# An attention kernel whose K transposes get their lead in units 19 to 22 instead of 10 to 16, with a shorter warm-up

## The chip, the cores and the metric

One NeuronCore of one Trainium2 chip. The metric is the device time of one execution in microseconds (us). Every run also lists the span of the core, which is some 1.8 us shorter, and the mean granted clock of TensorE (PE), the share of full speed that it was given. "VectorE" is DVE in the profile, "ScalarE" ACT, "GpSimd" POOL.

## The reference, cut to what matters

```python
B, Sq, D = 8, 112, 640
H, Sk, Dh = 32, 512, 192                 # all bfloat16
q = (x @ wq).reshape(B, Sq, H, Dh).transpose(0, 2, 1, 3)
p = softmax(einsum("bhqd,bhkd->bhqk", q, k_cache) * Dh ** -0.5)
o = einsum("bhqk,bhkd->bhqd", p, v_cache)
return o.transpose(0, 2, 1, 3).reshape(B, Sq, H * Dh) @ wo
```

K and V are 50 MB each and are read once; the whole program reads 117.5 MB.

## The kernel before

It works in 64 units: 8 groups of 4 heads, times 8 batches. A unit is a score block S (96 matmuls), the transposes T of the output of the unit two before, and PV of the unit before. In two slots per unit, (i, 0) ahead of PV and (i, 1) behind it, stands dense work: Q projections of the next group, or output projections O. `halves` cuts one in two: over both slots of a unit, or over slot 1 and slot 0 of the next unit. VectorE transposes K, four quarters per unit, and adds the O results up. GpSimd copies V and reorders the Q weights. In the code below cuts are marked `# ...`; conditions for the first and last units are left out as well.

```python
    WARM, WN, BRIDGE, RAW = 7, 100, 4, 4
    # ... slots of group 0, and of the last group:
            put(6, 0, ("O", 0, 2))
            put(7, 1, ("O", 0, 3))
    # ...
            halves(i0 + 1, 0, ("O", g - 1, 5))
            put(i0 + 2, 0, ("O", g - 1, 6), FRONT)
            put(i0 + 3, 0, ("O", g - 1, 6), BACK)
    # ... how many quarters are transposed by the end of unit i: the lead is the min(5, ...)
        want = min(4 * (i + 2) + min(5, 1 + max(0, i - 8) // 2), 4 * NU)
    # ... VectorE, unit i
                for it in kts[:2]:
                    do_KT(*it)             # waits for all of K of its unit at its first quarter
                do_OEs(i, 0)               # adds of the O that ended in slot (i, 0)
                for it in kts[2:3]:
                    do_KT(*it)
                do_NM(i - 1)               # normalization
                do_OEs(i, 1)
                for it in kts[3:]:
                    do_KT(*it)
    # ... PE, first half of a projection: its two PSUM banks must have been read out
                        if q == 0:
                            bank_free(pe, pair, h)
                    if c == 0:             # first Q projection of a group: all its weights reordered
                        W(pe, gW, DC * g)
    # ... GpSimd: when the weights of group g >= 2 are reordered; then middle(u + NM) copies V
                    at.setdefault(8 * (g - 1) - 5 + dc if g >= 2 else -1, []).append((g, dc))
    # ... PE, before everything: a warm-up, and a bridge over a wait for ScalarE
            for j in range(WARM + 1):
                (held if j else pe.matmul)(ps[:, 7, 0:4 * WN], wt[:], warm, True, True)
            # ...
            for j in range(BRIDGE):
                (held if j else pe.matmul)(ps[:, 7, 0:128], wt[:], wt[:], True, True)
```

Of the kernel before, what the change touches and what calls it, by code (L numbers as in the profile page):

```python
# [666 lines left out]
def build_main(nc, x, k_cache, v_cache, wq, wo, out, flag, regs, hints):  # L667
# [4 lines left out]
    NU = NG * B  # L672
# [11 lines left out]
    RW = DH + 2  # L684
    FULL, FRONT, BACK = range(3)
    FILL = {}
    WARM, WN, BRIDGE, RAW = 7, 100, 4, 4
    HINT_AT = {"act": 55, "dve": 54, "pool": 40, "sp": 56}
    NM = 2
    KP = [4] * NU  # L690
# [63 lines left out]

    kt_ahead, done = [], 4
    for i in range(NU + 2):
        want = min(4 * (i + 2) + min(5, 1 + max(0, i - 8) // 2), 4 * NU)
        kt_ahead.append((done, want))
        done = max(done, want)

# [566 lines left out]
def bass_standalone__mha_block_cached__near_ridge_kernel(  # L1327
    nc: bass.Bass,
    x: bass.AP,
    k_cache: bass.AP,  # L1330
    v_cache: bass.AP,
    wq: bass.AP,
    wo: bass.AP,
    out: bass.AP,
):
    with nc.sbuf_tensor("flag", [1, 1], I32) as flag:
        regs, hints = {e: nc.alloc_register(e, "raised") for e in mybir.ALL_ENGINES}, {}
        build_main(nc, x, k_cache, v_cache, wq, wo, out, flag, regs, hints)
        for e, loc in hints.items():
            nc.engines[e].br_eq(regs[e], 0, on_true="main_end", on_false="main_again").branch_hint(loc)  # L1340
        with nc.body("main_again"):
            nc.all_engine_barrier()
            build_mha_kernel(nc, x, k_cache, v_cache, wq, wo, out)
            nc.br("main_end")
        nc.switch_bb("main_end")
    return nc
# [28 lines left out]
```

## Time and profile before

| | |
|---|---|
| time before, three runs known at the prediction | 393.70, 394.04, 394.27 us |
| span of the profiled execution | 392.8 us |
| granted clock | 1.00 |
| DMA share of most slices | 0.9 or more until 370 us |

The windows view gives the engines' busy time in stretches: start and end, length, then PE, weight loads (PEld), VectorE, ScalarE and GpSimd, each with its count of instructions in brackets, then the granted clock, the DMA share and GB/s. Besides the start and the end, these are the stretches of the kernel before in which PE is clearly not full.

```profile
50.00:60.00 10.00, 8.74 (x255) 6.54 (x246) 8.54 (x16) 5.97 (x13) 4.95 (x10) 1.00 0.97 322
100.00:110.00 10.00, 9.43 (x234) 5.58 (x217) 8.26 (x18) 4.70 (x11) 4.19 (x10) 1.00 1.03 358
360.00:370.00 10.00, 9.05 (x253) 6.23 (x241) 9.16 (x18) 6.25 (x14) 4.43 (x9) 1.00 0.98 341
```

What to see: PE is full nearly everywhere, and the change aims at the middle row, whose 9.43 hides one hole of 0.9 us.

### The profile page before, as it was taken

The numbers are of one execution on the slowest core, as the hardware profiler recorded it, in microseconds if no ns is written. First come the engines' busy times: TensorE is split into PE (matmuls) and PEld (weight loads), VectorE is DVE, ScalarE is ACT, GpSimd is POOL, SyncE is SP. The second block draws the span as 40 slices with busy tenths as digits, with TensorE's granted clock in tenths as the row PEclk, the third lists the DMA queues.
The fourth block names the chain that finished last, engine by engine and source line by source line (L and its number), as shares of the span: only waits on it lengthen the run. The fifth ranks groups of instructions, "written<-read, shape, count | busy, mean of one in ns | idle before, by whom it ended". The sixth has DMA issues, their size and how long they took to land.

```text
span 392.8 us, 19830 instructions
## 1 busy us (share of the span) xinstructions
PE 386.1 (98%) x8836; PEld 243.8 (62%) x8286; DVE 284.1 (72%) x506; ACT 250.5 (64%) x550; POOL 152.7 (39%) x352
## 2 busy tenths in 40 slices
PE   8999989999999999999999999999999999999997
PEld 4556666666566666666666656656666666666664
DVE  1666688688797777776787776876678676789835
ACT  3767755766556765666845666566774766666662
POOL 5442544335343354234342255233454233233331
PEclk9999999999999999999999999999999999999999
DMA  8999999999999999999998999989998889989812
GB/s 259 379 369 362 350 318 349 334 324 300 356 356 305 326 304 341 370 293 319 352 331 287 281 327 330 343 266 312 311 336 291 252 270 301 349 259 321 276 38 70
DMA packets 88584, 120.00 MB, mean 305 GB/s; under 512 B 9776, under 2 KB 88496, under 8 KB 88496
## 3 DMA queue, kind: packets, MB, share of 16 engines
q1 hardware_dynamic: 88496, 118.72, 90.8%
q8 instruction: 68, 1.11, 1.2%
q14 instruction: 20, 0.16, 0.1%
HBM read 117.54 MB, written 1.15 MB: 302 GB/s over the span
## 4 chain that ended last, share of the span: by engine, by line
PE 90%; DMA 5%; DVE 2%; issue 1%; ACT 0%; SPq 0%; DVEq 0%
PE ps L933 20%; PE ps L972 20%; PE ps L858 20%; PE ps L954 20%; PE ps L983 6%; DMA kr<-in_k_cache_dram 5%; PE ps L892 2%; DVE kt L1111 2%; DMA xs<-in_x_dram 1%; PE ps L877 1%; PE ps L854 1%; DVE acc L1131 0%; PE ps L897 0%; DVE acc L1134 0%; SPq L1314 0%
## 5 line engine op out<-in xcount | busy, mean ns | idle before, releaser
L1111 DVE STREAM_TRANSPOSE kt<-kr 128x384 int32<-128x384 int32 x256 | 196.2, 870 | 13.2 <-DMA kr<-in_k_cache_dram 13.1
L1052 ACT ACTIVATE pT<-ps 128x448 bf16<-128x448 f32 x256 | 130.8, 561 | 83.8 <-PE ps L954 83.8
L954 PEld LDWEIGHTS ps<-qT,kt 32*128 32x128 bf16 x6144 | 77.2, 93 | 31.3 <-issue 21.8
L933 PE MATMUL ps<-wos,oT 128*128 128x320 bf16 (+2 forms) x342 | 93.2, 299 | 0.5 <-DVE acc L1134 0.5
L972 PE MATMUL ps<-vm,pT 128*128 128x193 bf16 x768 | 91.5, 247 | 1.0 <-ACT oT L1069 0.8
L858 PE MATMUL ps<-wos,oT 128*128 128x320 bf16 x330 | 91.2, 299 | 0.1
L954 PE MATMUL ps<-qT,kt 32*128 32x112 bf16 x6144 | 88.1, 208 | 1.4 <-issue 1.1
L1231 POOL TENSOR_SCALAR bad<-rinv 112x4 f32<-112x4 f32 x64 | 14.6, 228 | 188.8 <-DVE rinv L1117 188.8
L1214 POOL COPY vm<-vs 128x1152 int32<-128x1152 int32 x64 | 73.4, 1147 | 26.2 <-issue 18.0
L972 PEld LDWEIGHTS ps<-vm,pT 128*128 128x128 bf16 x768 | 67.9, 97 | 22.0 <-ACT oT L1069 11.6
L933 PE MATMUL ps<-xT,wqs 128*128 128x448 bf16 x210 | 74.0, 352 | 0.0
L858 PE MATMUL ps<-xT,wqs 128*128 128x448 bf16 x210 | 73.9, 352 | 0.0
L1059 ACT ACTIVATE os<-ps,rinv 112x192 bf16<-112x192 f32 x128 | 47.8, 435 | 29.7 <-DVE rinv L1117 29.7
L972 PE MATMUL ps<-vs,pT 128*128 128x193 bf16 x256 | 62.6, 245 | 0.0
L933 PEld LDWEIGHTS ps<-wos,oT 128*128 128x128 bf16 x342 | 33.2, 97 | 43.8 <-issue 36.1
L1036 ACT ACTIVATE qT<-ps 128x448 bf16<-128x448 f32 x96 | 47.8, 554 | 17.8 <-PE ps L933 13.1
L1134 DVE TENSOR_TENSOR acc<-ps,acc 128x320 f32<-128x320 f32 x84 | 37.3, 485 | 25.1 <-PE ps L933 25.1
L1069 ACT ACTIVATE oT<-ps 128x672 bf16<-128x672 bf16 x64 | 46.4, 726 | 2.1 <-PE ps L983 2.1
L1117 DVE RECIPROCAL rinv<-ps 112x4 f32<-112x4 f32 x64 | 11.1, 173 | 47.5 <-PE ps L972 47.4
L933 PEld LDWEIGHTS ps<-xT,wqs 128*128 128x128 bf16 x210 | 20.4, 97 | 34.0 <-issue 29.1
L1120 DVE TENSOR_TENSOR os<-ps,rinv 112x384 bf16<-112x384 f32 x64 | 35.7, 558 | 7.4 <-DVE rinv L1117 0.5
L1207 POOL COPY wqs<-wqr 128x384 bf16<-128x384 bf16 x70 | 33.2, 506 | 5.0 <-DMA wqr<-in_wq_dram 5.0
(44 smaller groups left out, 155.7 us busy)
## 6 DMA issues: line engine op xcount, KB each, us to landing
kr<-in_k_cache_dram SPq DMA_DIRECT2D x256, 192.0 KB, 4.2
vs<-in_v_cache_dram SPq DMA_DIRECT2D x256, 192.0 KB, 4.0
wos<-in_wo_dram SPq DMA_DIRECT2D x48, 160.0 KB, 4.6
wqr<-in_wq_dram SPq DMA_DIRECT2D x35, 192.0 KB, 5.2
wqs<-in_wq_dram SPq DMA_DIRECT2D x5, 192.0 KB, 4.3
out_dram<-xs SPq DMA_DIRECT2D x6, 160.0 KB, 2.0
xs<-in_x_dram SPq DMA_DIRECT2D x2, 320.0 KB, 3.7
xs<-in_x_dram SPq DMA_DIRECT2D x1, 480.0 KB, 5.8
```

The lines of the kernel that those rows point to most:

```text
L858: return pe.add_instruction(mybir.InstMatmult(name=nc.get_next_instruction_name(), engine=mybir.EngineType.PE, ins=[pe.lower_ap_or_imm(rhs ...
L933: mm = (pe.matmul if h == hs[0] and f == 0 else held)(ps[:, bank_of(pair, h), cs], w, rhs[h][:, cs], q == 0, q == n - 1 and f == cuts - 1)
L954: mm = pe.matmul(ps[:, a, SQ * t:SQ * (t + 1)], kt[u % NT][p, t, c // 2, :, c % 2], qT[g % 2][p, c, SQ * b:SQ * (b + 1)], start=(c == 0), ...
L972: mm = pe.matmul(pv[:, k, e, 0:DH + 1], pT[u % 2][:, a, t, :], src[:, a, v0:v0 + DH + 1], start=(t == 0), stop=(t == 3), skip_group_check= ...
L1036: act.activation(qT[g % 2][:, c, HQ * h:HQ * (h + 1)], ps[:, bank_of_Q0(n) if g == 0 else 6 + h, 0:HQ], ACTF.Copy).then_inc(aQ, 1)
L1052: act.activation(pT[u % 2][:, a, :, 0:SQ], ps[:, a, 0:4 * SQ].rearrange("p (t q) -> p t q", t=4), ACTF.Exp, scale=scale).then_inc(aEX, 1)
L1059: ins = act.activation(os_[u % 2][:, DH * (2 + e):DH * (3 + e)], pv_of(u)[0:SQ, 1, e, 0:DH], ACTF.Copy, scale=rinv[:, u % 4, 2 + e:3 + e])
L1069: act.activation(oT[:, :, SQ * b:SQ * (b + 1)].rearrange("p (k c) q -> p k c q", k=2), src.rearrange("p k (c q) -> p k c q", c=3), ACTF.Co ...
L1111: dve.transpose(dst, src).then_inc(vKT, 1)
L1120: dve.tensor_tensor(os_[u % 2][:, 0:2 * DH].rearrange("p (e d) -> p e d", e=2), pv[0:SQ, 0, :, 0:DH], rinv[:, u % 4, 0:2][:, :, None].broa ...
L1134: ins = dve.tensor_tensor(ob[:, m, cs] if g == NG - 1 else acc[:, m, cs], src, acc[:, m, cs], op=ALU.add)
L1214: gp.tensor_copy(vm[u % NM][:].rearrange("p a (t w) -> p a t w", w=RW)[:, :, :, 0:DH].bitcast(I32), vs[u % NV][:, :, 32:32 + 3 * DH].rearr ...
```

## The change

The lead is how many quarters of K, beyond those of the next unit, VectorE has transposed. The intent is to raise it later, when K is well ahead, and to trim the warm-up.

```diff
-    WARM, WN, BRIDGE, RAW = 7, 100, 4, 4
+    WARM, WN, BRIDGE, RAW = 5, 128, 3, 4
...
-        want = min(4 * (i + 2) + min(5, 1 + max(0, i - 8) // 2), 4 * NU)
+        want = min(4 * (i + 2) + min(5, 1 + max(0, i - 18)), 4 * NU)
```

## The prediction

> **What bounds the kernel now.** I read the page first: its busy shares, its chain of work and its DMA rows.
>
> ```profile
> span 392.8 us, 19830 instructions
> ...
> PE 386.1 (98%) x8836; PEld 243.8 (62%) x8286; DVE 284.1 (72%) x506; ACT 250.5 (64%) x550; POOL 152.7 (39%) x352
> ...
> PE 90%; DMA 5%; DVE 2%; issue 1%; ACT 0%; SPq 0%; DVEq 0%
> ...
> L1111 DVE STREAM_TRANSPOSE kt<-kr 128x384 int32<-128x384 int32 x256 | 196.2, 870 | 13.2 <-DMA kr<-in_k_cache_dram 13.1
> ```
>
> TensorE (PE) has work for 386.1 of 392.8 us, at granted clock 1.0 throughout, and 90% of the chain is its matmuls. The matmuls are full: the timeline has the 320-column ones 0.135 us apart, which is 320 columns at 2.4 columns per ns. The change touches none of that work, so it can only win or lose in the small holes. The sum of the holes is an upper bound: 392.8 - 386.1 = 6.7 us, and most of that is start, end and fixed turns. The last row is what the change moves: 256 K transposes on VectorE (DVE), 4 per unit, about 0.77 us apart (4 take 3.0 us), with 13.1 us of DVE idling until K data lands.
>
> Next I took the windows view in 10 us stretches to find where PE is less than full: 8.48 in 0 to 10, 8.74 in 50 to 60, 9.43 in 100 to 110, 9.05 in 360 to 370, and 9.9 or more everywhere else. Then the timeline of each. The one in 100 to 110 lies in unit 15, where the old rule has just raised the lead to 4:
>
> ```profile
> 102.62 1.60 DVE L1111 STREAM_TRANSPOSE kt<-kr 128x384 int32<-128x384 int32 x2
> ...
> 105.13 1.57 DVE L1111 STREAM_TRANSPOSE kt<-kr 128x384 int32<-128x384 int32 x2 [0.91 <-DMA kr<-in_k_cache_dram]
> ...
> 106.34 0.24 PE L972 MATMUL ps<-vs,pT 128*128 128x193 bf16 x1
> 106.56 0.86 DVE L1134 TENSOR_TENSOR acc<-ps,acc 128x320 f32<-128x320 f32 x2
> ...
> 107.08 0.10 PEld L933 LDWEIGHTS ps<-wos,oT 128*128 128x128 bf16 x1 [0.72 <-DVE acc L1134]
> 107.08 0.31 PE L933 MATMUL ps<-wos,oT 128*128 128x320 bf16 x1 [0.49 <-DVE acc L1134]
> 107.35 0.83 DVE L1111 STREAM_TRANSPOSE kt<-kr 128x384 int32<-128x384 int32 x1
> 107.47 0.30 PE L858 MATMUL ps<-wos,oT 128*128 128x320 bf16 x1
> 107.61 0.30 PE L933 MATMUL ps<-wos,oT 128*128 128x320 bf16 x1
> ```
>
> Read it as a relay. DVE is free at about 104.2 but stands before two transposes of unit 17 whose K only lands at 105.1. Behind them in its order is the output add (L1134) that empties the two PSUM banks of one output projection; its input was ready at about 105.1, when PE finished that projection. The add therefore runs at 106.56 rather than 105.1, and PE, done with PV at 106.43, cannot begin the next projection, which uses the same banks. A lead meant to protect PE has made PE wait.
>
> [...] the ready add stood 1.4 us behind a transpose waiting for data. [...] That bears on three holes in the middle of a score block (near 362.7, 368.2 and 373.7), which the trace files under issue: 0.44 and 0.47 us in the chain for the first two. Blocks of 16,384 bytes arrive on the instruction queue, one landing at 362.05, shortly before the first. It fits, but the trace does not prove it. [...] Here matmuls start at 0.99, and the pitch of 128-column ones falls from 107 to 56 ns at 5.7 us[...].
>
> **The change part by part.**
>
> *Lead.* Up to unit 9 both rules give a lead of 1; from unit 22 on both give 5. Between, the old one rises by one every second unit from 10 to 16; the new one stays at 1 to unit 18, then adds a fifth transpose in each of units 19 to 22. No transpose is added or removed: 256 times about 0.77 us stay, and the ordering of ACT, POOL and the DMA queue is unchanged. Only DVE's order moves.
>
> (a) Removed: the hole in unit 15. Normal turn from PV to projection is 0.08 us (100.04 to 100.12 one unit earlier); here 106.34 to 107.08 is 0.74, so 0.66 too many. Normal pitch is 0.135; 107.08 to 107.47 is 0.39, so 0.255 too many. Sum: **0.91 us**. With the lead at 1, unit 15 begins with transposes of unit 16, whose K landed at 99.1; three transposes from 102.6 end at about 104.95, just before the add is ready at 105.1. The add is through at about 106.0, before PV ends at 106.43. I expect all 0.91 back.
>
> (b) Lost slack in units 13 to 24. From the transpose and score starts I computed when each unit's last transpose ends against its score block's start. The old rule has 3 to 8 us there. With lead 1 the slots repeat those of units 8 to 10, with 2.6, 1.6 and 0.5 us to spare (score blocks at 61.04, 67.61, 73.04). The same slot pattern recurs in units 16 to 18, so the least slack should be about 0.5 us, at unit 18: thin, but no wait.
>
> (c) Supply. The queue's long issues are not waits for buffers: all four quarters of a unit carry the same condition, and often it is the third that takes 1.3 to 2.5 us after the first two went in 0.43 each. From 75 to 118 us nothing but 0.04 us lies between issues, so the queue is full and K lands at its own pace whatever the lead. K of units 20, 21, 22, 23 lands at 120.3, 127.1, 132.9, 137.6 us. With the new rule their first transposes come at about 125, 129, 135 and 138.5 us: later than the data every time. Buffer releases come later too, but estimated from the score starts they still precede the issue: unit 18's last transpose at about 119.6, the load that needs its buffer at 120.16. Nothing lost, half a microsecond of margin.
>
> (d) Six score blocks (19 to 24) regain a wait for the transposes. Blocks that already have it, such as 16 to 18, start with the same 98 ns turn as those without. Zero.
>
> *Warm-up.* Before: 8 matmuls of 400 columns, 3200 columns, 333 ns each, ending at about 3.63. After: 6 of 512, 3072 columns, 128 columns or 0.107 us fewer at the same rate. The first x rows reach the transposes at 4.37 in either case: hidden. Bridge: one of four 128-column matmuls goes, 0.056 us. But the projection after it loads its weights at 6.40 because ScalarE's copy of x ends at 6.33; the bridge ends at about 6.30. Hidden too. The only risk is that the clock's rise comes later.
>
> Sum: -0.91 + 0 + 0 = -0.9 us, so 394.04 - 0.9 = **393.1 us**, 0.2%.
>
> **The rivals.** First, *the hole moves*: the ramp in 19 to 22 makes DVE wait for K again (old rule: K slack 0.02 us at units 22 and 24), pushing an add or a normalization behind it. For it: 5 transposes per unit and a DVE busy near 0.75. Against: PE has 8 us of K slack there in the old kernel, and the adds of those units have a Q projection between them, not two projections back to back. Cost if it happens: up to 0.9, time about 394.0. Second, *PE waits for transposes at 16 to 18* because the slack is too thin: 0.3 to 1 us over these blocks, time 393.4 to 394.0. Third, *the gain is swallowed later* by the 360 to 376 us holes, if these depend on absolute timing or on where the instruction blocks fall: the stream shifts by a few instructions. They total about 1.5 us, so this could go either way by 0.5 us. Fourth, *the start*: a later clock rise costs half of the delay; 1 us later is 0.5 us.
>
> **Range and chances.** The three old runs spread over 0.57 us. With that, the third rival's half microsecond and a chance of one in five that rival one or two takes back much of the 0.9, I put 8 in 10 on 392.5 to 393.9. Two per cent is 7.9 us, more than all holes together (6.7), so faster is nearly excluded; slower would need the clock to stay low for 16 us.
>
> **What would show it.** Right: no hole above 0.2 us between 100 and 112 us; DVE's idle for K falling from 13.1 towards 9.3 us (what is left without the five waits of 0.76, 0.33, 1.36, 0.91 and 0.43 us at units 14 to 18); about 9.9 of PE in that stretch; all later score blocks some 0.9 us earlier. Wrong: a DVE release before a score block in units 16 to 20, DVE waiting for K at 21 to 24 with a PE hole behind it, the pitch of 128-column matmuls falling later than 5.7 us, or larger holes after 360 us.

## The result, and the profile after

Six runs of the changed kernel have a median of 394.1 us (392.85 to 394.99); six runs of the kernel before, 394.15 (392.39 to 394.49). The ratio is 1.0004, interval 0.998 to 1.0029: the same, where 0.9 us faster was predicted, and outside the stated range. (A ratio is the mean time of one kernel's runs over that of the other's of the same rounds, so not quite the ratio of the medians quoted.)

In the profiled execution the hole is gone. The page of the changed kernel:

```profile
span 392.2 us, 19832 instructions
...
PE 385.1 (98%) x8833; PEld 242.8 (62%) x8286; DVE 283.2 (72%) x506; ACT 250.4 (64%) x550; POOL 152.8 (39%) x352
...
PE 96%; DMA 1%; issue 1%; DVE 0%; SPq 0%; ACT 0%
...
L1111 DVE STREAM_TRANSPOSE kt<-kr 128x384 int32<-128x384 int32 x256 | 195.2, 871 | 12.0 <-DMA kr<-in_k_cache_dram 12.0
```

VectorE in unit 15 of the changed kernel, from the timeline:

```profile
102.09 2.27 DVE L1111 STREAM_TRANSPOSE kt<-kr 128x384 int32<-128x384 int32 x3
104.61 0.89 DVE L1134 TENSOR_TENSOR acc<-ps,acc 128x320 f32<-128x320 f32 x2 [0.25 <-PE ps L933]
```

The three transposes end before the add is ready; the add now waits 0.25 us for PE instead of PE for the add. The windows of the changed kernel show where the time went instead:

```profile
100.00:110.00 10.00, 10.00 (x261) 6.24 (x240) 8.27 (x16) 5.04 (x12) 5.39 (x12) 1.00 0.99 326
360.00:370.00 10.00, 8.33 (x249) 6.17 (x241) 8.44 (x17) 5.42 (x13) 3.60 (x8) 1.00 0.92 306
```

PE wins 0.57 us in the first row and has 0.72 us less in the second, against the rows before. The timeline of PE in the second stretch:

```profile
361.33 0.37 PE L954 MATMUL ps<-qT,kt 32*128 32x112 bf16 x13
362.88 0.82 PE L954 MATMUL ps<-qT,kt 32*128 32x112 bf16 x52 [1.18 <-issue]
```

A score block stops after its 13th record and goes on over a microsecond later, for nothing that a semaphore explains ("issue"). The kernel before has such a hole at the same place in the program, of half the size. So there were three questions: is the hole of unit 15 in every execution of the kernel before; what are the "issue" holes; and does the warm-up cost anything? The rival theories were: **A**, the hole belongs to the old lead always and its gain is eaten elsewhere; **B**, it was an accident of one execution; **C**, instruction blocks that arrive late scatter the time; **D**, the trimmed warm-up takes the gain back.

### The profile page after: what moved, and what is told of

The parts are those of the page before. It is cut to its first block, busy times and chain, and to the rows that moved or that the text cites. A ratio compares the mean times of both kernels' runs of the same rounds, so it can differ in the third digit from the quotient of the medians.

```text
span 392.2 us, 19832 instructions
## 1 busy us (share of the span) xinstructions
PE 385.1 (98%) x8833; PEld 242.8 (62%) x8286; DVE 283.2 (72%) x506; ACT 250.4 (64%) x550; POOL 152.8 (39%) x352
## 3 DMA queue, kind: packets, MB, share of 16 engines
q8 instruction: 68, 1.11, 1.2%
## 4 chain that ended last, share of the span: by engine, by line
PE 96%; DMA 1%; issue 1%; DVE 0%; SPq 0%; ACT 0%
PE ps L933 22%; PE ps L972 22%; PE ps L858 22%; PE ps L954 21%; PE ps L983 6%; PE ps L892 2%; DMA wqs<-in_wq_dram 1%; PE ps L877 1%; SPq L1314 0%; PE ps L897 0%; PE ps L854 0%; DVE kt L1111 0%; DVE acc L1131 0%; ACT oT L1069 0%; ACT pT L1052 0%
```

## The experiments

Each kernel left a trace and, unless told otherwise, six timed runs beside eleven or twelve of the kernel before on the same chip. A hole is the time from one matmul's start to the next, less its columns at 2.4 per ns (in the first trace 320 columns took 0.135 us); small fixed turns are left out.

### The kernel before once more

No edit.

> The kernel before, unchanged, run against itself: what noise is, and a second trace of it. Theory A (the hole in unit 15, some 0.9 us, belongs to the old lead in every execution): the second trace has it again, 0.6 to 1.0 us at unit 15. Rival B (it was an accident of one execution): the second trace has under 0.3 us there. Theory C (instruction blocks that arrive late in the short units near 360 us scatter the time): holes of 0.3 to 1.4 us inside score blocks after 355 us, of other sizes than 0.65, 0.68 and 0.26 us. Time within 0.3% of itself, single runs spread over 1.5 to 2 us.

Measured: 393.19 us median (392.72 to 394.68); against itself 1.0002, interval 0.9977 to 1.0027. Its trace has **no hole at unit 15**. It has one at unit 8 that the first trace lacks, 0.75 us by the matmul pitch, before the first Q projection of group 2. Timeline, GpSimd and then PE:

```profile
63.55 1.14 POOL L1214 COPY vm<-vs 128x1152 int32<-128x1152 int32 x1 [2.58 <-issue]
64.64 0.96 POOL L1207 COPY wqs<-wqr 128x384 bf16<-128x384 bf16 x2
```

```profile
64.83 0.24 PE L972 MATMUL ps<-vs,pT 128*128 128x193 bf16 x1
65.65 0.36 PE L933 MATMUL ps<-xT,wqs 128*128 128x448 bf16 x1 [0.58 <-POOL wqs L1207]
```

GpSimd copies V of unit 8 at once when it lands, and only then reorders the last piece of the weights that PE stands before. Theory A's "every execution" has fallen. VectorE in unit 15 of this trace, with the same order of instructions as in the first, shows why:

```profile
102.66 2.97 DVE L1111 STREAM_TRANSPOSE kt<-kr 128x384 int32<-128x384 int32 x4
105.47 0.87 DVE L1134 TENSOR_TENSOR acc<-ps,acc 128x320 f32<-128x320 f32 x2
```

K of unit 17 landed 1.52 us after score block 15 had begun, before VectorE asked for it at 2.2 us; in the first trace it landed at 3.27 us.

### One part at a time

Lead only: the second line of the diff above, with the old warm-up. Warm-up only: the first line, with the old lead. Each was run twice, and the changed kernel, unedited, twice more.

> The new lead with the old warm-up. Theory A: no hole at unit 15, 0.5 to 0.9 us faster than before over five rounds. Rival D (the lead gains but the new warm-up takes it back): faster by 0.5 us or more here while the warm-up alone is slower by as much. Rival C (late instruction blocks near 360 us take it back): no hole at unit 15, but holes after 355 us that are larger than in the kernel before; time within 0.4 us of before.

Measured: 392.93 us median (391.67 to 394.13), ratio 0.9994 (0.9968 to 1.002). No hole at unit 15; "issue" holes after it of 0.2 us in sum, the least but one of all these traces; span 390.7.

> The new warm-up with the old lead. My prediction: nothing, within 0.2 us. Rival D: slower by 0.5 us or more, with the clock's rise or the first score block later than the 13.2 us of both traces so far. The hole at unit 15 stays under theory A.

Measured: 393.36 us median (392.75 to 397.88), ratio 1.0029 (0.9988 to 1.007). First score block at 13.18 us, as in the kernel before. No hole at unit 15, though it has the old lead: again against A.

> The changed kernel again, for its noise and a second trace. Theory A: no hole at unit 15. Rival C: holes inside score blocks after 355 us of 1 to 2 us in sum, as in the first trace (1.39 and 0.69), against 1.6 in the kernel before. Time within 0.3 us of before, as measured already.

Measured: 394.81 us median (393.65 to 395.59), ratio 1.0038 (1.0012 to 1.0063): slower than before, which no theory but D had as likely. But its trace shows the first score block at 13.05 us, and "issue" holes in units 0, 5, 24, 46 and 60.

> The new lead with the old warm-up, again. Theory B (the hole of unit 15 falls in about one execution in four and is worth 0.9): faster by 0.2 us in the mean, that is within 0.5 us of before and not slower. Rival: the new lead itself costs; slower by 0.3 us or more.

Measured: 393.38 us (391.95 to 394.81), ratio 0.9995 (0.9965 to 1.0026).

> The new warm-up with the old lead, again. Rival D (the trimmed warm-up costs some 0.7 us in the mean though no trace shows where): slower than before by 0.4 to 1 us once more. If the first result (0.8 us, one run of 397.9 with a clock of 0.996 in it) was chance: within 0.35 us.

Measured: 393.67 us (393.05 to 394.92), ratio 1.0013 (0.9985 to 1.0041).

> The changed kernel a third time, on the chip of the other two. Rival D: as slow as the warm-up alone, 0.4 to 1.3 us above before, and the new lead alone is not. If neither part costs anything: within 0.35 us, and the 1.3 us of its second run was chance.

Measured: 393.77 us (392.74 to 396.88), ratio 1.0028 (0.9991 to 1.0065).

What follows: the new lead neither costs nor clearly gains (two ratios, both some 0.05% below 1, intervals of about 0.3% to either side). The kernels with the new warm-up came out above 1 every time. Over all runs, the changed kernel and the warm-up alone have a mean of 394.24 us in 30 runs; the kernel before and the new lead alone, 393.46 in 69: 0.8 us, with an interval from resampling of 0.3 to 1.3. One of the 30, the warm-up's run of 397.88 us, had a granted clock of 0.996; without it the difference is 0.7 us. No trace shows where it comes from.

### The columns and the instruction count of the warm-up, parted

```diff
-    WARM, WN, BRIDGE, RAW = 7, 100, 4, 4
+    WARM, WN, BRIDGE, RAW = 6, 114, 2, 4     # 3192 columns, three instructions fewer
+    WARM, WN, BRIDGE, RAW = 8, 85, 3, 4      # the other kernel: 3060 columns, the old count
+    WARM, WN, BRIDGE, RAW = 0, 16, 4, 4      # a third: next to no warm-up
```

> The old lead; warm-up of the old length (3192 columns instead of 3200) but with three PE instructions fewer before the first score block, as the new warm-up has. The kernels with the new warm-up average 0.8 us above the old ones (30 runs against 58), in all runs together, and no trace shows where. If it is where the blocks of 256 instructions fall that costs: slower than before by 0.5 to 1.2 us. If it is the 128 columns fewer: within 0.4 us.

Measured: 393.69 us (391.65 to 396.47), ratio 1.0007 (0.9969 to 1.0045).

> [...] If the columns cost (a start that is later in some executions): slower than before by 0.5 to 1.2 us. If where the instruction blocks fall costs: within 0.4 us. If both this and the other are within 0.4 us, the 0.8 us were chance or come from something I haven't tried.

Measured: 393.6 us (392.35 to 394.41), ratio 0.9996 (0.997 to 1.0023).

> The old lead with next to no warm-up: one matmul of 64 columns. If the start's warm-up matters at all (rival D), taking nearly all of it away shows it much larger than trimming 4%: transposes of x at half rate until later, the first score block 0.5 to 2 us later than 13.0 to 13.5, time slower by as much. If the start is set by the arrival of the first weights, the first score block stays within 0.3 us and the trimmed warm-up can cost nothing.

Measured: 394.96 us (393.7 to 395.58), ratio 1.0039 (1.0016 to 1.0062). First score block at 14.24 us, a good 1 us later than in all other traces (12.85 to 13.51). So the warm-up as a whole is worth 1.0 us at the start; theory D asks for 0.8 from trimming 4% of it. Neither of the two kernels that change one thing shows it, so D's cost is **not settled**: chance, or something of the two together that was not tried.

### The hole amplified: an earlier ramp, and none

```diff
-        want = min(4 * (i + 2) + min(5, 1 + max(0, i - 8) // 2), 4 * NU)
+        want = min(4 * (i + 2) + min(5, 1 + max(0, i - 8)), 4 * NU)
+        want = min(4 * (i + 2) + 1, 4 * NU)     # the other kernel
```

> The old warm-up, with the lead raised one quarter per unit in units 9 to 12, when K arrives just in time. If an early ramp makes VectorE stand before K that has not landed and so delays output adds (the mechanism I read in the first trace), this amplifies it: VectorE's idle for K over 15 us, one to three holes at units 10 to 16 of 0.5 us or more, 0.7 to 2 us slower. If that hole was an accident of when data came, and not the ramp's: no such holes, within 0.4 us of before.

Measured: 394.59 us (393.41 to 396.02), ratio 1.0021 (0.9996 to 1.0047), so likely slower but not clear of noise. VectorE's idle for K is 20.8 us, the most of all, and the hole of unit 15 is there again, at 1.81 + 0.26 us:

```profile
106.30 2.23 DVE L1111 STREAM_TRANSPOSE kt<-kr 128x384 int32<-128x384 int32 x3 [2.51 <-DMA kr<-in_k_cache_dram]
108.38 0.86 DVE L1134 TENSOR_TENSOR acc<-ps,acc 128x320 f32<-128x320 f32 x2
```

```profile
107.02 0.24 PE L972 MATMUL ps<-vs,pT 128*128 128x193 bf16 x1
108.91 0.31 PE L933 MATMUL ps<-wos,oT 128*128 128x320 bf16 x1 [1.64 <-DVE acc L1134]
```

The mechanism of the prediction is real: an add behind a transpose that waits for K. It only needs K later than the old lead usually finds it. How much of the 2.07 us is the ramp's doing is not shown: the ramp puts three transposes ahead of the add instead of two, but K of unit 17 also landed 3.76 us after score block 15 in this trace, later than in any trace with the old lead.

> The lead stays at 1 to the end. If the lead only matters once the last units become short (from unit 56 on, where VectorE needs about 4.6 us per unit and TensorE 4.1 to 4.9): no hole of the K kind in units 9 to 55, but PE waits for transposes in units 58 to 63, 1 to 3 us slower. If the lead is not needed at all: within 0.4 us of before, and the whole question of when to raise it is empty.

Measured: 394.31 us (393.42 to 396.49), ratio 1.0018 (0.9994 to 1.0043), the same within noise by its interval. Score blocks 58 to 63 start 0.06 to 1.33 us after their last transpose (3.9 to 6.9 in the kernel before), and one hole of 0.72 us stands before score block 60. "Issue" holes in units 22, 23 and 52 to 54 make up 2.5 us of this one trace. So in these runs the lead matters little even at the end.

### Instruction blocks

Counting PE's records (matmuls, weight loads and its sequencer's) in program order gave the clue. In twenty traces there are 60 holes of 0.14 us or more at position 192 or 193 of a count that wraps at 256; the large ones elsewhere have a named releaser, as at units 8 and 15. The page of either kernel's first trace counts 68 packets on the instruction queue q8, 1.11 MB; in the trace each is 16,384 bytes, and they come a median of 5.6 us apart. PE has some 17,180 records there, about 67 times 256. So I take one packet for one block of 256 records of PE's program, and call the passing of that position of the count a block turn. All 31 stalls of 0.3 us or more, in nineteen traces, were followed one by one: the fetch began 2.1 to 3.8 us after the preceding block turn, took 0.9 to 2.3 us, and the matmuls went on 1.2 to 1.6 us after its end. A late start is common: over all block turns before 355 us of the twenty traces its median is 2.1 us. My reading is that it becomes a stall when PE reaches the next turn first. Units 58 and 59 hold half a projection each, and such a unit lasts 4.1 us: less than the least of that sum, 2.1 + 0.9 + 1.2 = 4.2 us.

The test: no data for the last units. Its output is wrong, which doesn't matter for the time.

```diff
-    KP = [4] * NU
+    KP = [4] * 60 + [0] * (NU - 60)
...
-                if u < NU:
+                if u < 60:
                     load_k(u)
-                if u - 1 >= 3:
+                if 3 <= u - 1 < 60:
                     load_v(u - 1)
# and GpSimd's wait for V, from unit 60 on, is that of four units before
```

> The kernel before without the K and V loads of units 60 to 63, which then work on old buffers: a wrong result on purpose. Theory C (PE's instruction blocks queue behind data on the DMA engines, 2.5 to 3.4 us in the traces, which a unit of 4.1 us can't hide): fetches of blocks 61 to 64 start within 0.5 us of the block turn, no hole inside the score blocks of units 60 to 62, 0.5 to 1.6 us faster. If the fetches are late for a cause of their own: the starts stay 2 us or more behind the turn and the holes stay.

Measured in the trace: the fetches after block turns 61 to 64 began 0.8, 0.7, 0.0 and 0.3 us behind the turn, against 2.5, 3.4, 2.3 and 1.1 in the kernel before (1.6 to 3.4 at turns 61 and 62 in all nine other traces with the old lead), and score block 60 runs through:

```profile
361.60 1.36 PE L954 MATMUL ps<-qT,kt 32*128 32x112 bf16 x96
```

Against 13 + 52 + more records with 1.18 us in between above. By this one trace theory C is shown for these holes: with the data of the last units gone, the fetches began 0.0 to 0.8 us behind the turn, and score block 60 had no stall. The gain in time is not: the mean span of its four runs, 391.4 us, is that of the kernel before (391.6). Its time reads 396.1, but 4 to 5 us of it lie outside the span, and no trace shows them; I don't use it.

A second way to the same end is to take away the short units. One projection moves from unit 55 into unit 56, and the next ones each one unit later, so that units 58 and 59 hold a whole one:

```diff
-            put(i0 + 7, 1, ("O", g, 3))
+            if g < NG - 2:
+                put(i0 + 7, 1, ("O", g, 3))
...
-            halves(i0, 0, ("O", g - 1, 4))
-            halves(i0 + 1, 0, ("O", g - 1, 5))
-            put(i0 + 2, 0, ("O", g - 1, 6), FRONT)
-            put(i0 + 3, 0, ("O", g - 1, 6), BACK)
+            for m in range(4):
+                halves(i0 + m, 0, ("O", g - 1, 3 + m))
```

> The kernel before with one output projection (group 6, block 3) moved from unit 55 into unit 56, the next ones each one unit later, so that units 58 and 59 hold a whole one instead of half of one and no unit is 4.1 us short. Theory C (the holes after 360 us are instruction blocks of 256 that arrive some 4.7 us or more after the last one was begun, so that only short units run dry): the holes of units 60 to 62 go, 0.5 to 1.5 us faster than before. If those holes come from something else in the last units: they stay, within 0.4 us.

(The 4.7 us are an estimate from the traces up to then. In the first traces of the two kernels the matmuls behind the holes near 361 to 374 us went on 4.8 to 5.6 us after the block turn before.)

Measured: 393.21 us (392.81 to 394.84), ratio 1.0 (0.9977 to 1.0024). The holes of units 60 to 62 are gone; one of 0.71 us stands in unit 59 and one of 0.22 in unit 44.

> The changed kernel with the same move. Theory C: 0.5 to 2 us faster than the changed kernel alone, and the holes of units 60 to 62 gone. Otherwise as the changed kernel, 0 to 0.4% slower than before.

Measured: 393.05 us (392.96 to 394.44), ratio 1.0004 (0.998 to 1.0027). No hole after unit 42; 0.39 and 0.29 us in units 21 and 42. The holes left units 60 to 62 as theory C said, and the time did not follow: late blocks struck elsewhere, also in unit 59, which theory C had not said.

### A version that should have beaten both

All traces up to here have two fixed holes, 0.43 us before score block 7 and 1.0 us before PV of unit 6.

```diff
-            put(6, 0, ("O", 0, 2))
-            put(7, 1, ("O", 0, 3))
+            halves(6, 0, ("O", 0, 2))
+            halves(7, 0, ("O", 0, 3))
```

> The kernel before with the two projections of units 6 and 7 each cut in two halves around PV. All ten kernels' traces so far have a hole of 0.43 us before score block 7 (it waits for a transpose that stands behind an output add) and one of 1.0 us before PV of unit 6 (nothing left to fill in). If I read these two rightly, both shrink to under 0.2 us: 1.0 to 1.4 us faster. If DMA sets the pace of these units: the time comes back as K waits by unit 16, within 0.4 us.

Measured: 393.09 us (392.16 to 395.53), ratio 0.9993 (0.9968 to 1.0018). Both fixed holes shrank as read, and PE then stood 2.1 us at unit 8 before the same weight copy as in the second trace of the kernel before. What was gained before unit 8 was **given back at unit 8**: 0.46 us in a new hole before score block 8, 0.48 in a block stall inside it, and then the wait for the copy, since V of unit 8 doesn't land sooner (64.9 us in this trace, 63.1 in the first).

The new lead, the old warm-up, this edit and the moved projection together:

> New lead, old warm-up, projections of units 6 and 7 in halves, one projection moved from unit 55 to 56. Sum of what each should save in the mean: a quarter of 0.9 us (lead, one trace in four), 1.0 to 1.4 (units 6 and 7), 0.5 (units 58 to 62): 1.7 to 2.1 us, 0.4 to 0.5% faster than before, below the 2% of a verdict but clear of an interval of 0.25%. If the savings come back as other holes: within 0.3%.

Measured: 393.1 us (392.59 to 395.38), ratio 0.9987 (0.9967 to 1.0007). The trace lost 2.2 us at unit 8, and after that hole the clock fell:

```profile
66.00:70.00 4.00, 3.74 (x14) 0.74 (x13) 2.69 (x4) 0.74 (x3) 1.13 (x5) 0.57 1.00 337
```

The third number from the end is the granted clock, 0.57. The hole lasted from 63.95 to 66.26 us, less the 193 columns of one matmul, 2.2 us; from 66.26 to 69.59 us the 448-column matmuls then started 0.37 us apart, where those of the kernel before start 0.19 us apart. A hole of 2.1 us in another trace was not followed by such a fall; what decides it, these traces do not show. Then the same with GpSimd reordering one unit earlier:

```diff
-                    at.setdefault(8 * (g - 1) - 5 + dc if g >= 2 else -1, []).append((g, dc))
+                    at.setdefault(8 * (g - 1) - 6 + dc if g >= 2 else -1, []).append((g, dc))
```

> New lead, old warm-up, units 6 and 7 in halves, one projection moved to unit 56, and GpSimd reorders each group's Q weights one unit earlier. Theory G: in all traces with the old order the first Q projection of unit 8 starts when GpSimd's last weight copy ends (0.06 us after it in ten of fourteen), and that copy stands behind the V copy of unit 8, which waits for V to land at 62.9 to 65; so what is gained before unit 8 is lost there. Moved one unit earlier the copy ends before 61 us, the Q projection of unit 8 starts near 63.8 us without a wait, and the gain of units 6 and 7 stays: 1.5 to 2.5 us faster than before, interval clear of 1. If the gate is just the next data: Q starts at 65 us or later again, under 0.7 us.

Measured: 393.09 us (391.89 to 395.7), ratio 1.0001 (0.9967 to 1.0035). The gate opened: the weights were ready 5.9 us before PE came. But PE came no sooner than before, at 65.28 us, for a block stall took the place of the gate (lines of this kernel are numbered one lower):

```profile
59.40 0.86 PE L953 MATMUL ps<-qT,kt 32*128 32x112 bf16 x55
61.35 0.52 PE L953 MATMUL ps<-qT,kt 32*128 32x112 bf16 x28 [1.08 <-issue]
```

Units without their fixed waits are shorter, and the next block of instructions had begun to arrive only 3.7 us after the turn. No version here beats the kernel before beyond noise.

### One sum that all traces obey

| trace | span | Q projection of unit 8 starts | later holes with a named wait | later block stalls | rest |
|---|---|---|---|---|---|
| before | 392.8 | 65.6 | 0.9 (unit 15) | 1.6 | 324.7 |
| before, second | 391.6 | 65.7 | 0 | 1.2 | 324.7 |
| changed | 392.2 | 65.1 | 0 | 2.3 | 324.8 |
| changed, second | 392.6 | 66.2 | 0 | 1.5 | 324.8 |
| changed, third | 391.1 | 65.5 | 0 | 0.7 | 324.9 |
| lead only | 390.7 | 65.6 | 0 | 0.2 | 325.0 |
| lead only, second | 392.2 | 65.9 | 0 | 1.0 | 325.2 |
| warm-up only | 391.6 | 65.2 | 0 | 1.6 | 324.8 |
| warm-up only, second | 392.0 | 66.2 | 0 | 1.0 | 324.8 |
| earlier ramp | 394.2 | 66.0 | 2.1 (unit 15) | 1.4 | 324.7 |
| units 6 and 7 in halves | 393.8 | 67.1 | 0 | 1.8 | 324.9 |

The rest is the span less the three columns before it (holes of 0.14 us or more; in the trace whose clock fell, also less the 1.6 us lost at half rate). It lies between 324.7 and 325.2 in all twenty traces, also those not in the table. So executions differ in two things: when unit 8 begins its Q projection (65.1 to 67.1 us), and which blocks of instructions are late after it (0 to 2.5 us). What sets the first is not always the same: in 13 of the twenty traces PE waited there 0.2 us or more for the weight copy behind V; in the others, the first trace of either kernel among them, it came when the copy was done or just ending, and what it had lost before decided. No run shows that the change moves either of the two.

## Why the prediction was wrong, point by point

**The step that failed** is (a), "I expect all 0.91 back". It treated the hole of one profiled execution as a property of the kernel. Ten traces have the old lead: two of the kernel before, two with the trimmed warm-up, three with other warm-ups, two with moved projections and the one without the last loads. One of the ten has the hole. In the other nine K of unit 17 landed 0.97 to 2.20 us after score block 15 began, in that one 3.27, and VectorE asks at about 2.2. The eight traces with the new lead have none. So the term was one tenth of 0.91, about 0.09 us in the mean, an estimate from ten traces (it may be low: in the trace of the last version above, which has the new lead, K of unit 17 landed 3.75 us after score block 15, and the add did not wait); the two runs of the lead alone, at 0.9995 and 0.9994, neither show nor exclude it.

**The mechanism** in (a) was right. With the earlier ramp VectorE stood before K ahead of the same add, and the hole came back at twice its size.

**Steps (b) and (d) of the lead** held, and (c) in its outcome. Least slack of a score block was to be about 0.5 us at unit 18: measured 0.47, with 1.35 and 1.61 at units 16 and 17. K of units 20 to 23 landed at 119.9, 125.1, 131.0 and 136.1 us in the changed kernel, each before its first transpose (126.2, 131.2, 134.1, 139.8). But the margin of half a microsecond in (c) was not there. The DMA queue (SP) of the changed kernel, then VectorE:

```profile
117.97 0.42 SPq L1314 DMA_DIRECT2D wqr<-in_wq_dram  x1
119.17 1.75 SPq L1314 DMA_DIRECT2D kr<-in_k_cache_dram  x4
```

```profile
118.29 0.86 DVE L1111 STREAM_TRANSPOSE kt<-kr 128x384 int32<-128x384 int32 x1
```

The queue stood 0.78 us until the last transpose of unit 18 gave back the buffer that the load of K of unit 21 needs. All eight traces with the new lead have this wait at unit 21 (0.1 to 1.5 us), and none of the ten with the old lead, where the buffers of these units are free 1.5 us or more ahead. The six score blocks that regained a wait show no hole at their start. The first rival, the hole moving into the ramp, did not occur: no add there made PE wait. Block stalls of 0.2 to 0.7 us stand in units 21 to 24 in five of the eight traces with the new lead and in none of the ten with the old. The kernel without a ramp, which has the queue's wait too, has two (0.34 and 0.56 us), so they don't need the raising of the lead in units 19 to 22; whether the queue's wait causes them, no run isolates, and it stays open.

**VectorE's idle for K** was to fall from 13.1 to about 9.3 us. It was 12.0, 8.7 and 12.2 in the three traces of the changed kernel, and 11.2 in the second of the kernel before: the first units alone vary by that much, so it was no proof of anything.

**The warm-up's zero** held in every trace: first score block at 13.19, 13.05 and 12.86 us in the changed kernel, 13.18 and 13.02 in the kernel before. The fourth rival, a later rise of the clock, did not show: the pitch of the 128-column transposes had fallen (from 0.107 us to 0.056 in the kernel before) by 4.0, 5.9 and 5.7 us in these traces of the changed kernel, 5.7 and 5.8 in the kernel before. In the timed runs the new warm-up is 0.8 us slower, and that stays open.

**The third rival** was the right one to name and too small; its sign, larger holes after 360 us, came (1.39 us against 0.65). I gave the late holes 0.5 us either way and took them for a matter of the last units. Block stalls after unit 8 sum to 0.7, 1.5 and 2.3 us in three traces of the same changed kernel, and over all traces they stand in units from the first to the last but one.

**The range** came from three runs with a spread of 0.57 us. The 57 runs of the kernel before have a mean of 393.5 us, so that the base of 394.04 was itself 0.5 us high, a standard deviation of 0.84 us, and reach from 391.8 to 395.3. A gain of 0.9 us could hardly have been told in six runs even if real: from that deviation, the difference of two means of six has a standard error of 0.84 x sqrt(2/6) = 0.5 us.

## What to carry to other kernels

Before a hole is counted as a gain, ask what decides it: a fixed order of instructions, or a race between a landing and a request. Here the order was the same in ten traces, and the race gave the hole of 0.9 us, its releaser named, to one of them; so take a second trace of the same kernel first. In a kernel whose tensor engine is 98% busy, split the span into the last gate that data sets, the fixed work after it, and the holes after it; what was gained here ahead of the gate, at units 6 and 7, did not shorten the run (ratio 0.9993). And a hole with no releaser may be the program itself arriving late, as it was at the end of this kernel: count instructions and see whether the holes sit at one place of a block, as 60 did here at one position of 256.
